# First MLP of a three-stage kernel: raw words of w_out in their own place, its conversion a block sooner, and another spread of conversion steps

## The chip, the cores and the metric

The kernel runs on one core of a Trainium2 chip. The metric is the time on the device in microseconds, lower is better; before the change the median of three runs is 873.08 us (871.41 to 873.17).

## What is computed

Three stages follow each other: an attention with a memory (4 x 8 heads, 576 tokens, 64 wide), a first MLP with a softmax gate and a layer norm, and a second, gated MLP. The weights come as 64-bit floats. The change lies in the first MLP and in what is woven into it:

```python
h = x @ w_in                      # 2304 x 512 @ 512 x 1024
e = np.exp(h - np.max(h, -1))
solu = h * e / (e.sum(-1) + 1e-9)
ln = (solu - mu) / np.sqrt(var + 1e-6) * g_ln   # mu, var over the 1024
x = ln @ w_out                    # 1024 x 512
# second MLP
gate = 1 / (1 + np.exp(-(x @ w_gate)))
return (gate * (x @ w_val)) @ w_out2
```

## The kernel before

**The stages.** Attention ends at about 222 us, the first MLP (`Moe1.run`) lasts until 453 us, the second (`Moe2`) until the end. Matmuls run on a hi and a lo part of each operand (three matmuls for one), so each tile that TensorE (PE) reads is made by a copy that rounds (hi, on ScalarE, ACT) and a subtraction (lo, on VectorE, DVE, or GpSimd, POOL). [...]

**The first MLP.** 18 blocks of 128 tokens, t = 0 to 17; blocks 0 and 1 are begun within the attention's last steps by hooks (`hooks`, keys of a step in the attention's written order). From block 2 on the loop in `run` writes for block t, in this order: 24 matmuls `h` (L665) in two halves with the transposes `pl` of block t-2 (L712) between them; ACT's `parts(t-2, 0)` (L720), `norm(t-1)` (L702); DVE's `max` (L678); ACT's `exp` (L683); DVE's `parts(t-2, 1)` (L722, the lo part of lnT) and `mul` (L687 to L689); ACT's `square` (L694); and then products `po` (L731) of a group of three finished blocks with w_out, whose results go into X (L738). A half is 12 matmuls of 384 columns. `xsplit` (L652, L654) makes the x of a later block. Each engine works through its instructions in the order in which they are written. There are two buffers each for `h`, `pl` and `po`: `h(t)` waits for `square(t-2)`, `pl(t)` for the lo part of block t-1.

**w_out of the first MLP.** Eight row chunks c. 0 and 1 are converted in the attention (`ex16` to `ex19`), 2 to 7 by the five functions of `w_out` (load, one, two, three, four; lists `outs[c][0]` to `[4]`), one chunk in each block from 2 to 7, the last step (woh, L640, on ACT) a block after the others. All buffers of this conversion and of the second MLP's conversion (`raw`, `ex`, `M`, `hi`, `ho`) come from one pool `cv`. The tags `raw` of `rawwo2` and `rawwo3` lie where the attention's tiles were, and the loads wait until these are read for the last time.

**The second MLP's conversion.** 96 steps (`conv`) prepare its weights; they run in blocks 8 to 16 between the first MLP's own work: `later` holds the steps that are due, `go(n)` runs n of them. 16 come due at t = 8, then 10 in each block.

**The last part.** After block 17, `last()` does the remaining products, with the second MLP's first differences (L1008, POOL) and their hi and lo parts (L1018, L1022) beside them.

## Time and profile before

| | us |
|---|---|
| median of the runs shown | 873.08 (871.41 to 873.17) |
| profiled execution | 873.04 |
| its span | 871.2 |
| PE busy in the span | 839.7 (96%) |
| DVE busy | 640.4 (74%) |
| ACT busy | 501.5 (58%) |
| POOL busy | 483.4 (55%) |
| first MLP after the attention, blocks 2 to 8 | 82.66 |
| first MLP, blocks 9 to 17 | 113.55 |
| rest of the first MLP | 35.00 |

A stretch is read from the start of one matmul to the start of another. A time in brackets behind an instruction is the idle time of its engine ahead of it, with what ended it. PEclk is the granted clock of TensorE as a share of full speed; a matmul of a given shape that lasts about twice its usual time ran at the lower of the two levels.

### The profile page before, as it was taken

To read this page: it belongs to the slowest core of one execution; us is meant where nothing else is said; L and a number is where in the kernel's file an instruction comes from. 1 tells how busy PE (TensorE), PEld (TensorE's weight loads), DVE (VectorE), ACT (ScalarE), POOL (GpSimd) and SP (SyncE) were. 2 spreads that over 40 slices of the span, in tenths; PEclk is the share of its full clock that TensorE was granted. 3 is DMA by queue.
4 is the path that set the end of the run, shared out by engine and by line. 5 is a ranking of instruction groups with operands and counts; after the bars stand their busy time and mean duration, and the time that the engine had idled before them with its cause. 6 is when DMAs were issued, how large, how long until landed. Compare 5 with 4: busy or idle time off the path is not lost.

```text
span 871.2 us, 14952 instructions
## 1 busy us (share of the span) xinstructions
PE 839.7 (96%) x5020; PEld 734.0 (84%) x5020; DVE 640.4 (74%) x1406; ACT 501.5 (58%) x1089; POOL 483.4 (55%) x592
## 2 busy tenths in 40 slices
PE   6999999999799999999999999999999999999998
PEld 4777777777587887877998999899899999999997
DVE  7899999996688278889537778787876444846745
ACT  5899999996588367677633446435543223423221
POOL 5687777774265187768604775685566232432111
PEclk9899999999999899999999999999999999999999
DMA  6443434430121155655429875994799874291662
GB/s 148 108 107 88 115 92 119 100 78 14 61 73 53 46 176 178 210 186 170 145 83 393 253 283 176 378 406 142 242 409 303 282 214 123 96 381 53 220 251 97
DMA packets 132412, 153.56 MB, mean 176 GB/s; under 512 B 67184, under 2 KB 101232, under 8 KB 132336
## 3 DMA queue, kind: packets, MB, share of 16 engines
q1 hardware_dynamic: 132336, 152.61, 53.9%
q8 instruction: 40, 0.66, 0.3%
q14 instruction: 36, 0.29, 0.1%
HBM read 116.40 MB, written 36.18 MB: 175 GB/s over the span
## 4 chain that ended last, share of the span: by engine, by line
PE 72%; DVE 11%; ACT 7%; POOL 4%; issue 3%; DMA 2%; SPq 0%; POOLq 0%; DVEq 0%; ACTq 0%
PE s L1073 16%; PE acc L1126 16%; PE g L1073 8%; PE po L731 5%; PE x L503 5%; PE sc L394 4%; PE v L1073 4%; PE x L488 2%; ACT h L694 2%; PE sc L385 2%; ACT e L683 1%; DVE ex L130 1%; DVE ex L121 1%; DVE M L934 1%; POOL exwo L635 1%
## 5 line engine op out<-in xcount | busy, mean ns | idle before, releaser
L1126 PE MATMUL acc<-o,G 128*128 128x512 f32 x648 | 181.6, 390 | 0.2 <-DVE G L1092 0.2
L1111 POOL TENSOR_TENSOR vl<-vl,sg 128x384 f32<-128x384 f32 x36 | 37.1, 1029 | 206.4 <-ACT sg L1110 206.4
L1126 PEld LDWEIGHTS acc<-o,G 128*128 128x128 f32 x648 | 118.5, 188 | 10.2 <-DVE G L1092 0.7
L433 POOL TENSOR_SCALAR p<-p,first,cols 128x256 f32<-128x256 f32 (+3 forms) x142 | 92.0, 662 | 5.2 <-ACT ex L118 1.9
L665 PE MATMUL h<-wih,xs 128*128 128x512 f32 x288 | 86.9, 406 | 0.9 <-ACT h L694 0.9
L422 ACT ACTIVATE p<-p,nm 128x128 f32<-128x128 f32 (+2 forms) x144 | 82.7, 582 | 0.3 <-DVE nm L416 0.3
L731 PE MATMUL po<-lnT,woh 128*128 128x384 f32 x288 | 74.6, 340 | 3.7 <-ACT woh L640 3.7
L1103 ACT ACTIVATE sg<-sg 128x384 f32<-128x384 f32 x36 | 18.9, 525 | 93.9 <-DVE sg L1102 93.9
L1092 DVE TENSOR_TENSOR G<-vl,G 128x384 fp32r<-128x384 f32 x72 | 54.0, 750 | 21.5 <-ACT G L1089 21.4
L665 PEld LDWEIGHTS h<-wih,xs 128*128 128x128 f32 x288 | 53.7, 193 | 11.4 <-ACT h L694 1.3
L1089 ACT CAST G<-vl 128x384 fp32r<-128x384 f32 x72 | 37.0, 514 | 43.6 <-POOL vl L1111 34.8
L1110 ACT ACTIVATE sg<-sg 128x384 f32<-128x384 f32 x36 | 18.9, 526 | 71.0 <-DVE sg L1109 70.8
L731 PEld LDWEIGHTS po<-lnT,woh 128*128 128x128 f32 x288 | 53.0, 191 | 4.5 <-ACT woh L640 4.0
L416 DVE CUSTOM_DVE_ANT_0 p<-sc,mask 128x128 f32<-128x128 f32 (+3 forms) x128 | 54.6, 480 | 1.2 <-PE sc L394 1.0
L118 ACT ACTIVATE ex<-ex,consts 128x512 int32<-128x512 int32 (+1 forms) x56 | 36.2, 646 | 32.2 <-DVE ex L108 32.2
L121 DVE SCALAR_TENSOR_TENSOR ex<-raw,ex 128x512 int32<-128x512 int32 (+1 forms) x56 | 44.8, 799 | 7.6 <-ACT ex L118 7.6
L731 PE MATMUL po<-lnT,wol 128*128 128x384 f32 x144 | 48.9, 340 | 0.0
L906 POOL TENSOR_TENSOR M<-ex 128x256 f32<-128x256 f32 x48 | 41.0, 873 | 13.5 <-DVE ex L130 13.5
L1097 DVE TENSOR_TENSOR u<-s,p 128x384 f32<-128x384 f32 x36 | 20.0, 556 | 36.3 <-PE s L1073 34.7
L920 POOL TENSOR_TENSOR M<-M 128x256 f32<-128x256 f32 x48 | 45.5, 958 | 1.1
L341 POOL TENSOR_TENSOR G<-E,zm 128x640 f32<-128x640 f32 x16 | 25.0, 1563 | 37.3 <-DVE E L338 32.6
L665 PE MATMUL h<-wil,xs 128*128 128x512 f32 x144 | 45.7, 399 | 0.0
(711 smaller groups left out, 2485.3 us busy)
## 6 DMA issues: line engine op xcount, KB each, us to landing
o<-scro SPq DMA_DIRECT2D x36, 512.0 KB, 4.2
scrg<-hi SPq DMA_DIRECT2D x36, 256.0 KB, 4.7
scrg<-M SPq DMA_DIRECT2D x36, 256.0 KB, 4.7
raw<-in_moe_w_val_dram SPq DMA_DIRECT2D x12, 512.0 KB, 5.4
raw<-in_moe_w_gate_dram SPq DMA_DIRECT2D x12, 512.0 KB, 4.1
raw<-in_moe_w_out_dram SPq DMA_DIRECT2D x12, 512.0 KB, 5.3
scro<-ho SPq DMA_DIRECT2D x12, 512.0 KB, 2.7
out_dram<-X SPq DMA_DIRECT2D x18, 256.0 KB, 2.0
```

The source lines that it names most:

```text
L121: nc.vector.scalar_tensor_tensor(ex, raw[:, :, 1], -0x80000000, ex, ALU.bitwise_and, ALU.bitwise_or)
L416: nc.vector.tensor_tensor_reduce(p, x, m, -1.0, 3.0e38, ALU.add, ALU.min, nm)
L422: nc.scalar.activation(p, p, AF.Exp, bias=nm, scale=-1.0, accum_out=self.sum[n % 2][:, c, 0:1])
L433: eng.tensor_scalar(p, p, r["rs"][:, c : c + 1], og, ALU.mult, ALU.mult)
L503: nc.tensor.matmul(r["x", g][64 * hh : 64 * hh + 64, c0 : c0 + src.shape[1]], r["vt"][:, c : c + D], src, start=False, stop=j == 0,)
L665: lambda s=s, w=w, j=j: nc.tensor.matmul(ph[:, j * 512 : j * 512 + 512], xs[:, s, c], self.wi[c][w][:, j * 512 : j * 512 + 512], start=(c ...
L731: nc.tensor.matmul(self.po[g, m], w[:, m * P : m * P + P], L[x][c // 4][:, c % 4], start=(c == 0 and n == 0), stop=(c == NF1 - 1 and n == 2),)
L906: nc.gpsimd.tensor_mul(out[:, sl], m[:, sl], e[:, sl])
L920: ops[i][0](*ops[i][1:])
L1073: nc.tensor.matmul(po, W[:, a, c * P : c * P + P], xb[b][:, c], start=c + i == 0, stop=c == 1 and i == 2)
L1092: nc.vector.tensor_sub(G[:, 1, hs[h]], vl[:, h], f32(G[:, 0, hs[h]]))
L1126: nc.tensor.matmul(po, G[:, x, sl], o[:, w], start=first and i == 0, stop=stop and i == 2)
```

## The change

1. **Pools.** `cv` becomes three pools: `cm` for M, `cr` for raw, `cv` for the rest. rawwo2 and rawwo3 lie elsewhere, over other tiles of the attention.
2. **Conversion of w_out one block sooner.** `outs[2][1:4]` and `outs[3][1]` stand before the loop; block t has `outs[t][4]` behind its `max`, `outs[t+1][2]` and `[3]`, the load and `[1]` of t+2.
3. **Block 1.** Its max and exp hang on an earlier attention step, mul on another; `xsplit(2)` is split around block 0's mul and square.
4. **Order on DVE.** For t < 8 the lo part (L722 twice) of block t-2 stands ahead of `max(t)`, not behind `exp(t)`.
5. **Products of group 0.** c 0 to 4 in block 5, nothing in block 6, c 5 to 7 and the two other column blocks (48 matmuls) in block 7. Block 8 is then like the others.
6. **Spread of the 96 steps.** 14 come due at t = 7, then 8 or 9 in each of the blocks 8 to 17.

```diff
@@ Moe1.run
-            outs[2][1]()
             for n in range(2):
                 self.xsplit(NFIRST + 1, n)
+            for f in outs[2][1:4]:
+                f()
+            outs[3][1]()
...
-                if t >= NF1:
-                    n = min(len(conv), 16 + (len(conv) - 16) * (t - NF1) // (NBLK - NF1 - 2))
+                if t >= NF1 - 1:
+                    n = 14 + (len(conv) - 14) * (t - NF1 + 1) // (NBLK - NF1)
                     later += conv[done:n]
                     done = n
-                go(3)
+                if t >= NF1:
+                    go(3)
...
                 self.parts(t - 2, 0)
+                if t < NF1:
+                    self.parts(t - 2, 1)
                 if t > NFIRST:
                     self.norm(t - 1)
                 self.max(t)
-                if NFIRST < t < NF1:
-                    outs[t - 1][4]()
+                if t < NF1:
+                    outs[t][4]()
                 self.exp(t)
-                go(2)
-                self.parts(t - 2, 1)
+                if t >= NF1:
+                    go(2)
+                    self.parts(t - 2, 1)
...
-                if t < NF1:
-                    outs[t][2]()
+                if t + 1 < NF1:
+                    outs[t + 1][2]()
                 self.mul(t)
...
+                pieces = self.pieces(t)
+                if t == NF1 - 1:
+                    for f, copy in pieces[:4]:
+                        f(), copy and copy()
+                    pieces = pieces[4:]
                 self.square(t)
-                if t < NF1:
-                    outs[t][3]()
+                if t + 1 < NF1:
+                    outs[t + 1][3]()
                     if t + 2 < NF1:
-                        outs[t + 2][0]()
-                    if t + 1 < NF1:
-                        outs[t + 1][1]()
+                        outs[t + 2][0]() if t + 2 > 3 else None
+                        outs[t + 2][1]()
@@ pieces
+            if t == 5:
+                return [(lambda m=m: self.product(0, m, list(range(5))), None) for m in range(2)]
+            if t == NF1 - 1:
                 return [
+                    *((lambda m=m: self.product(0, m, [5, 6]), None) for m in range(2)),
+                    *((lambda m=m: self.product(0, m, [7]), lambda m=m: self.result(0, m)) for m in range(2)),
+                    *self.halves(0)[4:],
+                ]
@@ hooks
-                lambda: m1.max(0, A), lambda: m1.exp(0, A), split(2),
-                lambda: [f(0, A) for f in (m1.mul, m1.square)], lambda: m1.norm(0),
+                lambda: m1.max(0, A), lambda: m1.exp(0, A), lambda: m1.xsplit(2, 0, A),
+                lambda: m1.mul(0, A), lambda: m1.square(0, A), lambda: m1.xsplit(2, 1, A),
             ],
+            (NP, "cv_b"): [lambda: m1.max(1, A), lambda: m1.exp(1, A)],
+            (NP, "x0_c"): [lambda: m1.mul(1, A), lambda: m1.norm(0)],
...
-            for f in (m1.max, m1.exp, m1.mul, m1.square):
-                f(1, A)
+            m1.square(1, A)
@@ pools
-        with pool("cv", side="right") as cv:
+        with pool("cm", side="right") as cm, pool("cr", side="right") as cr, pool("cv", side="right") as cv:
+            cv = Pools(M=cm, raw=cr, ex=cv, hi=cv, ho=cv)
```

On DVE, around block 1's maximum (`h1`, reduced by L678 into `first`; `wo0` is the converted w_out chunk 0, `X` the attention's output), the rows before are:

```order
L121 SCALAR_TENSOR_TENSOR ex17_3530<-raw17_3492,ex17_3530 128x256
L130 SCALAR_TENSOR_TENSOR ex17_3530<-raw17_3492,consts_63,ex17_3530 128x256
L144 COPY X_67<-x15_0_3588 128x4x64
L557 TENSOR_TENSOR wo0_74<-ex16_3527,wo0_74 128x256
L557 TENSOR_TENSOR wo0_74<-ex17_3530,wo0_74 128x256
L144 COPY X_67<-x15_1_3595 128x5x64
L678 TENSOR_REDUCE first_103<-h1_3549 128x1
L687 TENSOR_REDUCE first_103<-first_103 128x1
L688 RECIPROCAL first_103<-first_103 128x1
L689 SCALAR_TENSOR_TENSOR e1_3625,first_103<-h1_3549,first_103,e1_3625 128x1024
```

and after:

```order
L121 SCALAR_TENSOR_TENSOR ex17_3530<-raw17_3492,ex17_3530 128x256
L130 SCALAR_TENSOR_TENSOR ex17_3530<-raw17_3492,consts_63,ex17_3530 128x256
L678 TENSOR_REDUCE first_103<-h1_3549 128x1
L144 COPY X_67<-x15_0_3587 128x4x64
L687 TENSOR_REDUCE first_103<-first_103 128x1
L688 RECIPROCAL first_103<-first_103 128x1
L689 SCALAR_TENSOR_TENSOR e1_3612,first_103<-h1_3549,first_103,e1_3612 128x1024
L557 TENSOR_TENSOR wo0_74<-ex16_3527,wo0_74 128x256
L557 TENSOR_TENSOR wo0_74<-ex17_3530,wo0_74 128x256
L144 COPY X_67<-x15_1_3594 128x5x64
```

The maximum now stands directly behind chunk 0's last L130, `mul(1)` (L687 to L689) follows the first L144, and the two L557 and the second L144, which stood ahead of all four, come after them.

On DVE, at block 2 (`exwo2` and `exwo3` are chunks 2 and 3 of w_out in conversion, `rawwo` their raw words, `pl0` the transposes of block 0, `h2` the block's matmul result), the rows before are:

```order
L108 TENSOR_SCALAR exwo2_3728<-rawwo2_3724 128x512
L111 TENSOR_SCALAR exwo2_3728<-rawwo2_3724 128x512
L678 TENSOR_REDUCE consts_63<-h2_3734 128x1
L722 TENSOR_TENSOR lnT0_3747<-pl0_0_3748,lnT0_3747 128x4x128
L722 TENSOR_TENSOR lnT0_3747<-pl0_1_3753,lnT0_3747 128x4x128
L687 TENSOR_REDUCE consts_63<-consts_63 128x1
L688 RECIPROCAL consts_63<-consts_63 128x1
L689 SCALAR_TENSOR_TENSOR e2_3773,consts_63<-h2_3734,consts_63,e2_3773 128x1024
L121 SCALAR_TENSOR_TENSOR exwo2_3728<-rawwo2_3724,exwo2_3728 128x512
L130 SCALAR_TENSOR_TENSOR exwo2_3728<-rawwo2_3724,consts_63,exwo2_3728 128x512
```

and after:

```order
L108 TENSOR_SCALAR exwo2_3737<-rawwo2_3730 128x512
L111 TENSOR_SCALAR exwo2_3737<-rawwo2_3730 128x512
L121 SCALAR_TENSOR_TENSOR exwo2_3737<-rawwo2_3730,exwo2_3737 128x512
L130 SCALAR_TENSOR_TENSOR exwo2_3737<-rawwo2_3730,consts_63,exwo2_3737 128x512
L108 TENSOR_SCALAR exwo3_3746<-rawwo3_3732 128x512
L111 TENSOR_SCALAR exwo3_3746<-rawwo3_3732 128x512
L722 TENSOR_TENSOR lnT0_3762<-pl0_0_3763,lnT0_3762 128x4x128
L722 TENSOR_TENSOR lnT0_3762<-pl0_1_3768,lnT0_3762 128x4x128
L678 TENSOR_REDUCE consts_63<-h2_3749 128x1
L687 TENSOR_REDUCE consts_63<-consts_63 128x1
L688 RECIPROCAL consts_63<-consts_63 128x1
L689 SCALAR_TENSOR_TENSOR e2_3793,consts_63<-h2_3749,consts_63,e2_3793 128x1024
```

The whole of chunk 2's work and the first half of chunk 3's now stand ahead of the lo part of block 0, and the maximum of block 2 behind it.

On PE, from the end of block 7's second half on (`po0_0` to `po0_3` are group 0's four column blocks, `woh7` the hi part of chunk 7), the rows before are:

```order
L731 MATMUL po0_0_4000<-lnT0_3747,woh5_3714 128x384 x2
L731 MATMUL po0_0_4000<-lnT0_3747,wol5_3715 128x384
L731 MATMUL po0_1_4013<-lnT0_3747,woh5_3714 128x384 x2
L731 MATMUL po0_1_4013<-lnT0_3747,wol5_3715 128x384
L665 MATMUL h8_4174<-wih0_83,xs8_4072 128x512 x2
L665 MATMUL h8_4174<-wil0_84,xs8_4072 128x512 x2
L665 MATMUL h8_4174<-wih0_83,xs8_4072 128x512 x2
```

and after:

```order
L731 MATMUL po0_0_4018<-lnT0_3762,woh5_3720 128x384 x2
L731 MATMUL po0_0_4018<-lnT0_3762,wol5_3721 128x384
L731 MATMUL po0_0_4018<-lnT0_3762,woh6_3722 128x384 x2
L731 MATMUL po0_0_4018<-lnT0_3762,wol6_3723 128x384
L731 MATMUL po0_1_4034<-lnT0_3762,woh5_3720 128x384 x2
L731 MATMUL po0_1_4034<-lnT0_3762,wol5_3721 128x384
L731 MATMUL po0_1_4034<-lnT0_3762,woh6_3722 128x384 x2
L731 MATMUL po0_1_4034<-lnT0_3762,wol6_3723 128x384
L731 MATMUL po0_0_4018<-lnT0_3762,woh7_3724 128x384 x2
L731 MATMUL po0_0_4018<-lnT0_3762,wol7_3725 128x384
L731 MATMUL po0_1_4034<-lnT0_3762,woh7_3724 128x384 x2
L731 MATMUL po0_1_4034<-lnT0_3762,wol7_3725 128x384
```

Before, `h8` follows chunk 5. After, chunks 6 and 7 of the first two column blocks stand ahead of it, and behind these rows, still ahead of `h8`, all chunks of the third and fourth column block.

## Rows read from the trace of the kernel before

**Rows 1.** Stretches: from-to, length, PE, PEld, DVE, ACT, POOL busy, PEclk, DMA share.
```profile
222.19:304.85 82.66, 72.90 (x359) 63.56 (x357) 53.78 (x102) 56.13 (x94) 32.17 (x52) 0.94 0.18 58
304.85:418.40 113.55, 105.67 (x543) 92.36 (x543) 97.06 (x141) 78.75 (x138) 88.15 (x111) 0.98 0.56 179
418.40:453.40 35.00, 35.00 (x209) 34.94 (x209) 14.67 (x18) 16.50 (x28) 13.46 (x18) 1.00 0.30 100
```

**Rows 2.** PE in time: start, us, line, out<-in, count, [idle before <-releaser].
```profile
228.72 1.63 PE L712 MATMUL pl<-ident,e 128*128 128x128 f32 x8 [3.47 <-DVE e L689]
...
238.58 1.23 PE L712 MATMUL pl<-ident,e 128*128 128x128 f32 x8 [1.70 <-DVE lnT L722]
...
285.26 1.01 PE L731 MATMUL po<-lnT,woh 128*128 128x384 f32 x2 [3.69 <-ACT woh L640]
...
288.48 2.12 PE L731 MATMUL po<-lnT,wo 128*128 128x384 f32 x6
```

**Rows 3.** PE in time, second stretch; first three rows begin h9, products, h10.
```profile
304.85 0.63 PE L665 MATMUL h<-wih,xs 128*128 128x512 f32 x2
...
311.23 0.51 PE L731 MATMUL po<-lnT,woh 128*128 128x384 f32 x2
...
317.50 0.63 PE L665 MATMUL h<-wih,xs 128*128 128x512 f32 x2
...
333.96 1.41 PE L712 MATMUL pl<-ident,e 128*128 128x128 f32 x8 [2.08 <-DVE lnT L722]
335.01 1.20 PE L665 MATMUL h<-wih,xs 128*128 128x512 f32 x2
```

**Rows 4.** DVE in time around blocks 1 and 2.
```profile
219.02 0.48 DVE L130 SCALAR_TENSOR_TENSOR ex<-raw,consts,ex 128x256 f32<-128x256 uint16 x1
...
223.32 0.76 DVE L557 TENSOR_TENSOR wo<-ex,wo 128x256 fp32r<-128x256 f32 x2 [3.19 <-ACT wo L553]
...
224.40 1.22 DVE L678 TENSOR_REDUCE first<-h 128x1 f32<-128x1024 f32 x1
...
227.28 1.28 DVE L689 SCALAR_TENSOR_TENSOR e<-h,first,e 128x1024 f32<-128x1024 f32 x1
...
231.48 1.05 DVE L130 SCALAR_TENSOR_TENSOR ex<-raw,consts,ex 128x256 f32<-128x256 uint16 x1
...
235.94 0.43 DVE L108 TENSOR_SCALAR exwo<-rawwo 128x512 int32<-128x512 int32 x1 [1.70 <-DMA rawwo<-in_moe_w_out_dram]
...
240.71 0.80 DVE L121 SCALAR_TENSOR_TENSOR exwo<-rawwo,exwo 128x512 int32<-128x512 int32 x1
```

**Rows 5.** SP in time: where rawwo's loads are issued.
```profile
232.56 25.86 SPq L105 DMA_DIRECT2D rawwo<-in_moe_w_out_dram  x5
```

**Rows 6.** ACT in time: exp(2), exp(7), and woh7's cast.
```profile
237.87 1.11 ACT L683 ACTIVATE e<-h,consts 128x1024 f32<-128x1024 f32 x1 [3.11 <-DVE consts L678]
...
276.79 1.11 ACT L683 ACTIVATE e<-h,consts 128x1024 f32<-128x1024 f32 x1
...
284.59 0.62 ACT L640 CAST woh<-exwo 128x512 fp32r<-128x512 f32 x1 [1.35 <-POOL exwo L635]
```

**Rows 7.** The stretch from max(9) to max(16), columns as in rows 1.
```profile
316.78:410.56 93.78, 87.28 (x449) 76.44 (x448) 82.20 (x123) 66.60 (x117) 72.23 (x92) 0.98 0.60 194
```

**Rows 8.** DVE in time, second stretch.
```profile
316.78 1.21 DVE L678 TENSOR_REDUCE consts<-h 128x1 f32<-128x1024 f32 x1
...
320.10 1.27 DVE L722 TENSOR_TENSOR lnT<-pl,lnT 128x512 fp32r<-128x512 f32 x2
...
323.48 0.42 DVE L108 TENSOR_SCALAR ex<-raw 128x512 int32<-128x512 int32 x1
...
367.45 0.96 DVE L108 TENSOR_SCALAR ex<-raw 128x512 int32<-128x512 int32 x1
```

**Rows 9.** POOL's second difference T2 and ACT's cast of it, in time.
```profile
428.27 1.99 POOL L1008 TENSOR_TENSOR Tt<-X,Tt 128x384 f32<-128x384 f32 x2
...
432.47 0.85 ACT L1018 CAST xt2h<-Tt 128x768 fp32r<-128x768 f32 x1
```

More of the change, by code (lines that the diff above doesn't have):

```diff
@@ L767, in run @@
             for t in range(NFIRST, NBLK):
-                if t >= NF1:
-                    n = min(len(conv), 16 + (len(conv) - 16) * (t - NF1) // (NBLK - NF1 - 2))
+                if t >= NF1 - 1:
+                    n = 14 + (len(conv) - 14) * (t - NF1 + 1) // (NBLK - NF1)
                     later += conv[done:n]
                     done = n
-                go(3)
+                if t >= NF1:
+                    go(3)
                 mms = [f for c in range(NC) for f in self.h(t, c)]
-                at = len(mms) if t == NF1 else len(mms) // 2
-                for f in mms[:at]:
-                    f()
-                if t == NF1:
-                    outs[t - 1][4]()
-                    for f, copy in self.pieces(0):
-                        f(), copy and copy()
+                for f in mms[: len(mms) // 2]:
+                    f()
                 for x in range(2):
                     self.trans(t - 2, x)
-                for f in mms[at:]:
+                for f in mms[len(mms) // 2 :]:
                     f()
                 self.parts(t - 2, 0)
+                if t < NF1:
+                    self.parts(t - 2, 1)
                 if t > NFIRST:
@@ L800, in run @@
                     self.xsplit(t + 2, 1)
+                pieces = self.pieces(t)
[3 more added lines that the diff above has]
+                    pieces = pieces[4:]
                 self.square(t)
[L802 to L803 removed]
+                if t + 1 < NF1:
+                    outs[t + 1][3]()
                     if t + 2 < NF1:
[L805 to L808 removed]
+                        outs[t + 2][0]() if t + 2 > 3 else None
+                        outs[t + 2][1]()
+                for f, copy in pieces:
                     f(), copy and copy()
@@ L813, in pieces @@
         def pieces(self, t):
-            if t == 0:
+            if t == 5:
+                return [(lambda m=m: self.product(0, m, list(range(5))), None) for m in range(2)]
+            if t == NF1 - 1:
                 return [
-                    (lambda m=m: self.product(0, m, [6, 7]), lambda m=m: self.result(0, m)) for m in range(2)
-                ] + self.halves(0)[4:]
+                    *((lambda m=m: self.product(0, m, [5, 6]), None) for m in range(2)),
+                    *((lambda m=m: self.product(0, m, [7]), lambda m=m: self.result(0, m)) for m in range(2)),
+                    *self.halves(0)[4:],
+                ]
             if t < NF1:
-                cs = {5: list(range(4)), 6: [4], 7: [5]}.get(t)
-                return [(lambda m=m: self.product(0, m, cs), None) for m in range(2)] if cs else []
+                return []
             g, i = divmod(t - 5, GB)
@@ L1273, in pool, with tile @@
         return tc.tile_pool(name=nm, bufs=bufs, reuse_waits="tile", **kw)
+    class Pools(dict):
+        def tile(self, shape, dtype, tag, **kw):
+            return self[tag].tile(shape, dtype, tag=tag, **kw)
     scr = ctx.enter_context(tc.tile_pool(name="scr", bufs=1, space=bass.MemoryType.DRAM))
```

2 lines of the change are left out of this document (removed).

## The prediction

> **What bounds the kernel now.** I read first the busy table: PE is busy for 96% of the span, so only time that PE loses can be won. By the table of stretches it loses it in two places around the attention's end: 82.66 us in which PE is busy 72.90 at a granted clock of 0.94, and 113.55 us with 105.67 busy at 0.98; in the 35.00 us behind them it is busy throughout [rows 1]. To price PE's own work I take block 9, which waits for nothing: h9 starts at 304.85, its products at 311.23, h10 at 317.50 [rows 3]. So a block's 24 matmuls and its transposes cost 6.38 us, and three halves of products (36 matmuls) 6.27, or 0.174 apiece.
>
> The first stretch holds seven such blocks (h2 to h8) and 132 product matmuls: 7 x 6.38 + 132 x 0.174 = 67.6. PE loses 82.66 - 67.6 = 15.0 there. PE's rows in time show where [rows 2]: it waits 3.47 for DVE's mul(1), 1.70 for the lo part of lnT, and 3.69 for ACT's woh7, and matmuls behind the first and last of these are slow (six products in 2.12, against 6 x 0.174 = 1.04: the lower clock level). The rest is small waits and restarts.
>
> The second stretch reaches from h9's start to h17's end. Between two block ends PE has 6.38 and three halves (12.65), or two halves (6.38 + 4.18 = 10.56) in blocks 10, 13 and 16. Eight intervals, five long and three short, make 94.9; with h17's 6.38 it is 101.3, so PE loses 12.2. The loss is waits for lnT's lo part, the longest 2.08, with the next two h matmuls in 1.20 against 0.63 without the wait [rows 3]. What makes lnT late is DVE: from max(9) to max(16), seven blocks, it needs 93.78 us, 13.40 a block, and is busy for 82.20 of it [rows 7]. And 6.38 + 8 x 13.40 = 113.6 is the stretch's length: DVE's loop sets it.
>
> **Parts 1 to 4, the start.** DVE does block 1's max at 224.40, after it sat 3.19 in front of an L557 that waits for ACT; the mul ends at 227.28 + 1.28 = 228.56 [rows 4], and pl0 starts 0.16 later [rows 2]. In the new order the max can follow the L130 of 219.02 [rows 4], at 219.5. The chain from there to mul's end took 4.16, so mul ends at 223.7, before PE gets to pl0 (228.72 - 3.47 = 225.25). The 3.47 go, and the slow matmuls behind it.
>
> Next late is pl1. Before, it waits for L722 behind max(2), behind rawwo2's L108, which waited 1.70 for its load until 235.94 [rows 4]; that load was issued at 232.56 [rows 5], right when the L130 of 231.48 + 1.05 ended [rows 4], which had the old buffer. Moved, it waits for an attention matmul that ends by 222.2, so it lands before it is needed: 10 us sooner. DVE then has L557 and the conversions of w_out's chunk 1, which before lasted from 228.56 to the L557 that ended about 234.2, some 5.7. They start about 4 sooner, behind the two moved L557, so I take their end at 230.1. Six conversion instructions of rawwo2 and rawwo3 follow, four of about 0.4 and two up to 0.8 [rows 4]: until 233.2. Two L722 (1.2) and the max (1.2) end at 234.4 and 235.65, where exp(2) starts: 2.2 sooner than 237.87 [rows 6]. PE reaches pl1's place 5 us sooner and waits some 2.5 there, for DVE again; that is a new wait and stays inside the chain.
>
> From exp(2) to exp(7) the blocks come every (276.79 - 237.87) / 5 = 7.78 us [rows 6], and ACT is the engine that paces them: its work per block isn't changed, only the order. So I keep 7.78, and exp(7) starts at 274.55.
>
> **Parts 2 and 5, woh7.** Its cast now stands right ahead of exp(7), not at 284.59 behind the first steps of the second MLP's conversion and a wait for POOL of 1.35 [rows 6], so woh7 is there at 274.6 and the 3.69 shrink to a little. From it to h9's start PE has 6 + 48 + 36 product matmuls and h8: 90 x 0.174 + 6.38 = 22.0, with 0.6 for restarts: h9 starts at 297.2. Before: 304.85. **Gain 7.6.** Bounds: if exp(2) gets no sooner, h9 starts 2.2 later and 5.4 stay; if pl1's wait is gone too, 9. The seven casts (L640) stand ahead of an exp each, on ACT; exp waits if POOL's product is late.
>
> Part 5 costs PE nothing: the same matmuls, 48 of them ahead of h8 instead of behind. They hide the 14 conversion steps now at the end of block 7: 14 x 0.88 (below) = 12.3 on DVE, beside 48 x 0.174 + 6.38 = 14.7 on PE. Without that cover, max(8) is 12 later.
>
> **Part 6, the spread.** Of DVE's 13.40, the block's own work is the max (1.21) and the part from L722 to the end of xsplit (320.10 to 323.48, 3.38) [rows 8]: 4.59. The other 8.81 are ten steps: 0.881 apiece with their waits, or (82.20 / 7 - 4.59) / 10 = 0.715 without. Now 8.25 steps stand in a mean block: 4.59 + 8.25 x 0.881 = 11.86, against PE's 94.9 / 8 = 11.87. So DVE just stops being the bound. A single late block can be borne: L722 ends some 4.6 after the max starts, and PE asks for it two halves and half an h later, 4.18 + 2.8 = 7.0; that leaves 2.4 in the short blocks. The whole 12.2 could go. But the chunks of conversion aren't even, and DVE and PE run at the same pace, so I leave one wait like the longest (2.08), and half of what it drew after it, 1.2: **gain 8.9**, bounds 12.2 and, if a step gets dearer, below nothing.
>
> What a step costs depends on POOL. An L108 of the same shape takes 0.42 at 323.48 and 0.96 at 367.45 [rows 8]; a conversion's DVE instruction can be 0.54 longer. The Trainium skill (SBUF — State Buffer, "Who interferes with whom") says that DVE and GpSimd share a port pair which is an exclusive lock, and that a DVE instruction with two SBUF inputs contends with a GpSimd one that reads SBUF; by it, a denser loop on both engines would lengthen DVE's steps, and the gain could be lost as in the first rival below. The two L108 agree with that as far as they go. A step's price then lies between 0.715 and 0.881 + 0.54 = 1.42; I take 0.881, since POOL's work shrinks with the steps in a block as DVE's does.
>
> **The tail.** The 35.00 are full [rows 1]: nothing to win. To lose: steps now run in block 17, so POOL gets to T1 and T2 later; T2 ends at 430.26 and ACT casts it at 432.47 [rows 9], which leaves 2.2. I take 0.5, with 0 and 2 as bounds.
>
> **Sum.** 873.04 (the profiled run, as good as the median 873.08) - 7.6 - 8.9 + 0.5 = 857.0.
>
> **Rivals.** *DVE paces the second stretch still.* At a step of 1.1, midway to the upper bound, the loop is 13.67, 6.38 + 8 x 13.67 - 2.4 (slack) = 113.3, and only the start's gain is left: 873 - 7.6 - 0.3 + 0.5 = 865.7. For it: the long L108. Against: the mean that holds for seven blocks has such rows in it.
>
> *ACT takes the start's gain back.* If POOL's product ends after max(t), each exp waits behind its L640 as the last one did, 1.35 [rows 6]; five blocks make 6.75 of the 7.6: 863.9. It decides once POOL's product comes later than the max. Against: the product still has a whole block of time.
>
> *Slower.* DVE's step price again, but higher: from 4.59 + 8.25p = 14.57, p = 1.21, the second stretch loses the 7.1 that start and tail leave; that is six tenths of the steps' instructions moving from 0.42 to 0.96. At 1.3 the loop is 15.32 and the time 879. Against: it would be dearer than any mean here.
>
> *Nothing.* The start is only shifted and the loop paced as before: both of the first two rivals, 872.
>
> **Chances.** Forecast (853.5 to 861) 0.63, the DVE rival 0.14, the ACT rival 0.14, slower 0.04, nothing 0.05. A difference under 0.2%, 1.7 us, is no change for what can be measured here. So faster 0.91, same 0.05, slower 0.04. The range takes in the forecast with both gains in full (873 - 7.6 - 12.2 + 0.5 = 853.7) and the first two rivals: 853.5 to 866.
>
> **What would show it.** Of the changed kernel: no wait of PE for mul(1); rawwo2's load issued by about 222; exp(2) near 235.7 and exp(7) 38.9 later; no wait at woh7 over 1.5; h9 at 297. From max(9) to max(16) about 83 to 85 us, seven times 11.9, with PE waits for lnT of under 4 in sum. A loop of 12.7 or more a block, with L108 or L111 near 0.96 in most chunks, speaks for the DVE rival; exp(3) to exp(7) more than 8.5 apart, with ACT waiting for POOL at L640, for the ACT rival. I am wrong if h9 starts after 301, or if PE's waits in the last blocks move to the tail behind T1 or T2.

## The result and the profile after

The kernel after takes 859.46 us (median, 857.94 to 859.68), the kernel before 872.49 beside it; the ratio is 0.9848 (95% interval 0.9831 to 0.9865), a gain of 13.0 us. The forecast was 857.0 with a range of 853.5 to 866.

In the rows, the conversion steps are made of these lines, on tiles `ex` of 128x512: L108 and L111 take exponent and mantissa out of the raw words (DVE), L118 and a scaling turn them to floats (ACT), L121 and L130 put in sign and low bits (DVE), and POOL multiplies the two (L635 for w_out, L914 for the second MLP). From block 2's loop on, line numbers differ from those of the kernel before: POOL's products and sums L906 and L920 are L914 and L928 after, the lo part L934 is L942, and the differences L1008 and their casts L1018 are L1016 and L1026; in some of the runs below they move by a few lines more.

The busy table of the page and its row of TensorE's clock, after:

```profile
PE 834.7 (97%) x5020; PEld 731.9 (85%) x5020; DVE 631.7 (74%) x1406; ACT 501.0 (58%) x1089; POOL 481.7 (56%) x592
...
PEclk8899999999999999999999999999999999999999
```

The first MLP by stretches, after (columns as in rows 1: start of h2 to start of h9, to the first product behind h17, to the first matmul of the second MLP):

```profile
221.50:298.36 76.86, 70.95 (x359) 61.09 (x358) 58.36 (x105) 57.98 (x97) 44.37 (x66) 0.98 0.24 78
298.36:399.61 101.25, 101.25 (x541) 91.86 (x541) 79.92 (x133) 73.64 (x129) 69.40 (x92) 1.00 0.57 180
399.61:439.42 39.81, 36.95 (x209) 36.50 (x208) 17.39 (x22) 18.59 (x32) 19.93 (x24) 0.96 0.29 100
```

With the same marks the kernel before has 82.66, 113.36 and 35.09 [rows 1; there the last mark but one is 0.19 later]. So the start gains 5.80, the second stretch 12.11, and the tail loses 4.72. With 0.69 in the attention, which differs so from profile to profile (h2 starts between 220.7 and 222.8 in all of them), and 0.48 lost behind, this makes the 13.4 between the spans. The second stretch is full now: 101.25 busy of 101.25, which is the 101.3 that the prediction worked out as PE's own work.

All PE waits of 0.2 us or more from h2 to the end of the first MLP, after (start, us, line, [idle before <-releaser]):

```profile
234.11 1.71 PE L712 MATMUL pl<-ident,e 128*128 128x128 f32 x8 [3.23 <-DVE lnT L722]
...
240.07 0.74 PE L665 MATMUL h<-wih,xs 128*128 128x512 f32 x2 [0.48 <-ACT h L694]
...
247.76 0.73 PE L665 MATMUL h<-wih,xs 128*128 128x512 f32 x2 [1.01 <-ACT h L694]
...
275.27 0.62 PE L731 MATMUL po<-lnT,woh 128*128 128x384 f32 x2 [0.79 <-ACT woh L640]
...
276.09 0.44 PE L731 MATMUL po<-lnT,wol 128*128 128x384 f32 x1 [0.20 <-POOL wol L154]
...
277.26 1.32 PE L731 MATMUL po<-lnT,wo 128*128 128x384 f32 x6 [0.21 <-ACT X L738]
...
410.98 1.55 PE L731 MATMUL po<-lnT,wo 128*128 128x384 f32 x6 [2.86 <-ACT X L738]
```

The 3.47 for mul(1) and the 3.69 for woh7 [rows 2] are gone or 0.79, and the waits for lnT in the second stretch [rows 3] are gone altogether. Two long ones remain: 3.23 at pl1, and a new one of 2.86 in the tail, for a result copy (L738).

DVE in time at the start, after: max and mul of block 1, rawwo2's first conversion, two later instructions of rawwo2's and rawwo3's conversion, max(2).

```profile
218.72 1.22 DVE L678 TENSOR_REDUCE first<-h 128x1 f32<-128x1024 f32 x1
...
221.61 1.28 DVE L689 SCALAR_TENSOR_TENSOR e<-h,first,e 128x1024 f32<-128x1024 f32 x1
...
229.68 0.42 DVE L108 TENSOR_SCALAR exwo<-rawwo 128x512 int32<-128x512 int32 x1
...
230.89 0.69 DVE L121 SCALAR_TENSOR_TENSOR exwo<-rawwo,exwo 128x512 int32<-128x512 int32 x1 [0.45 <-ACT exwo L118]
...
232.51 0.95 DVE L111 TENSOR_SCALAR exwo<-rawwo 128x512 int32<-128x512 int32 x1
...
234.58 1.21 DVE L678 TENSOR_REDUCE consts<-h 128x1 f32<-128x1024 f32 x1
```

SP in time there, the issue of rawwo's loads:

```profile
218.54 0.85 SPq L105 DMA_DIRECT2D rawwo<-in_moe_w_out_dram  x2
```

ACT in time, exp(2) and exp(7):

```profile
235.82 1.11 ACT L683 ACTIVATE e<-h,consts 128x1024 f32<-128x1024 f32 x1 [1.13 <-DVE consts L678]
...
275.13 1.11 ACT L683 ACTIVATE e<-h,consts 128x1024 f32<-128x1024 f32 x1
```

Max(1) follows the last L130 directly and is 5.7 us sooner than in [rows 4] (5.0 counted from h2's start). The loads are issued at 218.54, not at 232.56 [rows 5], and DVE no longer waits for their words. Exp(2) stands at 235.82 (forecast 235.65), exp(7) at 275.13 (274.55), h9 at 298.36 (297.2).

DVE's maxima in the second stretch, after: of blocks 9, 10, 11, 13 and 16, then the step in front of the last, and max(17).

```profile
306.16 1.21 DVE L678 TENSOR_REDUCE consts<-h 128x1 f32<-128x1024 f32 x1
...
317.57 1.22 DVE L678 TENSOR_REDUCE consts<-h 128x1 f32<-128x1024 f32 x1 [2.13 <-PE h L665]
...
328.13 1.23 DVE L678 TENSOR_REDUCE consts<-h 128x1 f32<-128x1024 f32 x1 [1.05 <-PE h L665]
...
353.41 1.23 DVE L678 TENSOR_REDUCE consts<-h 128x1 f32<-128x1024 f32 x1 [2.99 <-PE h L665]
...
391.05 1.21 DVE L678 TENSOR_REDUCE consts<-h 128x1 f32<-128x1024 f32 x1
...
403.23 0.69 DVE L942 TENSOR_TENSOR M<-M,hi 128x512 fp32r<-128x512 f32 x1 [2.71 <-POOL M L928]
...
403.84 1.22 DVE L678 TENSOR_REDUCE consts<-h 128x1 f32<-128x1024 f32 x1
```

From max(9) to max(16) it takes 84.89 us, against 93.78 [rows 7]; and DVE now waits for PE in front of three maxima (2.13, 1.05, 2.99). Without these 6.17 its loop is (97.68 - 6.17) / 8 = 11.44 us. Less the block's own 4.59 [rows 8], that is 6.85 for some 8.13 steps (65 lie between max(9) and max(17)): 0.843 a step, where 0.881 was taken. DVE has stopped being the bound, except in block 17: there max(17) starts at 403.84 though h17 ended at 399.61.

Where the tail goes, after. First POOL in time, block 16's last small instruction and the conversion's sums:

```profile
399.19 0.77 POOL L698 TENSOR_SCALAR consts<-consts 128x1 f32<-128x1 f32 x1
...
401.76 2.75 POOL L928 TENSOR_TENSOR M<-M 128x256 f32<-128x256 f32 x3
```

Then ACT in time, square(17) and the copies behind it:

```profile
409.32 1.12 ACT L694 ACTIVATE h<-e,consts 128x1024 f32<-128x1024 f32 x1 [0.94 <-DVE e L689]
...
410.47 0.84 ACT L738 COPY X<-po 128x384 f32<-128x384 f32 x2
```

Three conversion steps stand ahead of max(17). The last of them waits 2.71 for POOL's sums (L928), which stand on POOL behind block 16's small L698 and a product. So max(17), mul(17) and square(17) are late; ACT copies the first result of block 17's products only behind square(17), at 410.47; and the products of the third column block, which need that PSUM buffer, wait for it.

### The profile page after: what moved, and what is told of

It is laid out like the page before. It is cut to its first block, busy times and chain, and to the rows that moved or that the text cites. A ratio compares the mean times of both kernels' runs of the same rounds, so it can differ in the third digit from the quotient of the medians.

```text
span 857.8 us, 14952 instructions
## 1 busy us (share of the span) xinstructions
PE 834.7 (97%) x5020; PEld 731.9 (85%) x5020; DVE 631.7 (74%) x1406; ACT 501.0 (58%) x1089; POOL 481.7 (56%) x592
## 4 chain that ended last, share of the span: by engine, by line
PE 78%; DVE 6%; ACT 5%; POOL 4%; DMA 4%; issue 2%; SPq 1%; POOLq 0%; ACTq 0%; DVEq 0%
PE s L1081 15%; PE acc L1134 15%; PE po L731 8%; PE g L1081 8%; PE h L665 6%; PE x L503 5%; PE sc L394 4%; PE v L1081 4%; PE x L488 2%; PE sc L385 1%; ACT h L694 1%; PE pl L712 1%; DMA raw<-in_moe_w_val_dram 1%; DMA gv0s<-scrg 1%; ACT e L683 1%
## 5 line engine op out<-in xcount | busy, mean ns | idle before, releaser
L914 POOL TENSOR_TENSOR M<-ex 128x256 f32<-128x256 f32 x48 | 41.8, 891 | 18.1 <-DVE ex L130 18.1
L118 ACT ACTIVATE ex<-ex,consts 128x512 int32<-128x512 int32 (+1 forms) x56 | 36.2, 647 | 22.7 <-DVE ex L108 22.7
L121 DVE SCALAR_TENSOR_TENSOR ex<-raw,ex 128x512 int32<-128x512 int32 (+1 forms) x56 | 41.6, 742 | 9.9 <-ACT ex L118 9.8
L928 POOL TENSOR_TENSOR M<-M 128x256 f32<-128x256 f32 x48 | 42.5, 896 | 1.2
```

What stands on the lines that cost most here:

```text
L121: nc.vector.scalar_tensor_tensor(ex, raw[:, :, 1], -0x80000000, ex, ALU.bitwise_and, ALU.bitwise_or)
L914: nc.gpsimd.tensor_mul(out[:, sl], m[:, sl], e[:, sl])
L928: ops[i][0](*ops[i][1:])
```

## The experiments

All times are medians beside runs of the kernel before, which stood at 872.2 to 872.5. The stretches of each run's profile, with the marks used above:

| kernel | time | start | second | tail |
|---|---|---|---|---|
| before | 872.5 | 82.66 | 113.36 | 35.09 |
| after | 859.46 | 76.86 | 101.25 | 39.81 |
| e1: no steps ahead of max(17) | 859.7 | 76.88 | 101.25 | 38.59 |
| e2: after, old spread | 866.46 | 76.90 | 113.33 | 35.08 |
| e3: before, new spread | 876.4 | 82.31 | 110.47 | 41.74 |
| e5: after, old block 1 | 862.87 | 80.87 | 101.26 | 39.77 |
| e6: after, one pool | 862.26 | 78.85 | 101.25 | 39.92 |
| e9: after, max ahead of lo | 860.2 | 75.78 | 101.26 | 41.00 |
| e11: after, woh casts on DVE | 858.62 | 76.13 | 101.25 | 38.25 |
| f1: last copy ahead of square(17) | 859.91 | 76.85 | 101.26 | 40.61 |
| f2: f1 and last lo parts on DVE | 857.72 | 76.88 | 101.25 | 37.57 |
| g1: f2, e9, e11 and products spread | 856.1 | 75.62 | 101.26 | 37.67 |
| e3b: before, 16 steps first | 876.36 | 82.23 | 111.24 | 42.14 |
| g2: after, no steps in block 7 | 871.01 | 76.85 | 111.97 | 40.32 |

In the kernels made from the kernel after, start and second stretch repeat to 0.1 us where an edit doesn't touch them, so they tell small effects apart that the medians, with runs some 1 to 3 us apart, don't. The tail doesn't repeat like that: where nothing in it was edited (after, e5, e6, e9, e11) it takes 39.81, 39.77, 39.92, 41.00 and 38.25, by the clock that follows the same wait (last section). So two tails of single profiles that are less than 2.8 apart say little by their length. In the kernels made from the kernel before, an untouched start differs by up to 0.4.

**The parts of the start.** First, part 3 undone (e5):

```diff
-            (NP, "cv_b"): [lambda: m1.max(1, A), lambda: m1.exp(1, A)],
-            (NP, "x0_c"): [lambda: m1.mul(1, A), lambda: m1.norm(0)],
...
-            m1.square(1, A)
+            for f in (m1.max, m1.exp, m1.mul, m1.square):
+                f(1, A)
```

> The kernel after with part 3 undone: block 1's maximum, exp and mul behind the conversions as in the kernel before, xsplit(2) not split. Theory (DVE's chain of mul(1), chunk 1's conversion, chunk 2's, L722, max(2) leads to exp(2), and ACT's pace of 7.8 us per block carries exp(2) on to h9): PE waits 3.5 for mul(1) again, exp(2) comes 3.8 later, at about 239.6, and so does h9; time 863.3. Rival (the wait of 3.23 at pl1, which stands behind it in the kernel after, takes it up): 859.5 to 860.

862.87. Its PE wait for mul(1), from PE in time:

```profile
228.57 1.84 PE L712 MATMUL pl<-ident,e 128*128 128x128 f32 x8 [3.47 <-DVE e L689]
```

And its max(2), from DVE in time:

```profile
238.92 1.21 DVE L678 TENSOR_REDUCE consts<-h 128x1 f32<-128x1024 f32 x1
```

The wait of 3.47 is back to the digit; counted from h2's start, max(2) comes 3.8 later than in the kernel after, as expected, and the start is 4.0 longer. The chain from mul(1) to exp(2) and on to h9 carries the whole delay, as the theory said; the wait at pl1 shrinks to 1.73 but doesn't take it up.

Part 1 undone (e6):

```diff
-        with pool("cm", side="right") as cm, pool("cr", side="right") as cr, pool("cv", side="right") as cv:
+        with pool("cv", side="right") as cv:
...
-            cv = Pools(M=cm, raw=cr, ex=cv, hi=cv, ho=cv)
```

> The kernel after with part 1 undone: one pool for all buffers of the conversions, so rawwo2 and rawwo3 lie where they did before. Theory: their loads are issued only when the last L130 of ex19 has ended, about 228.1, and land some 3.4 later, at 231.5; DVE wants the words at 229.7, so it waits 1.8 there, exp(2) and all behind it come 1.8 later, and the time is 861.3. Rival (DVE has other work or the load lands in time): 859.5.

862.26. The issue of rawwo's loads, from SP in time:

```profile
229.36 0.80 SPq L105 DMA_DIRECT2D rawwo<-in_moe_w_out_dram  x2
```

And the first conversion of them, from DVE in time:

```profile
232.89 0.43 DVE L108 TENSOR_SCALAR exwo<-rawwo 128x512 int32<-128x512 int32 x1 [1.84 <-DMA rawwo<-in_moe_w_out_dram]
```

Counted from h2's start, the load is issued 9.5 later than in the kernel after, and DVE waits 1.84 for it (1.8 expected); the start is 2.0 longer. The median is 2.8 above that of the kernel after, more than that: in the profile h2 starts 1.28 later, which differs so without any edit. So the start's 5.8 lose 4.0 without part 3 and 2.0 without part 1, each undone by itself; both lie on one chain, and the two needn't add. Parts 2 and 5, the earlier woh7, weren't run apart; what they bring by themselves stays open.

Part 4 undone (e9):

```diff
                 self.parts(t - 2, 0)
-                if t < NF1:
-                    self.parts(t - 2, 1)
...
                 if t >= NF1:
                     go(2)
-                    self.parts(t - 2, 1)
+                self.parts(t - 2, 1)
```

> The kernel after with part 4 undone: in blocks 2 to 7 the lo part of lnT (two L722) stands behind the maximum and exp again. Theory (exp(2) starts ACT's chain of 7.8 us per block, and the L722 stand in front of it): exp(2) comes 1.2 sooner, at about 234.6, h9 too, though PE waits 1.2 longer at pl1: 858.3. Rival (PE, which waits for the L722 at pl1, is the one that carries the delay on): h3 ends 1.2 later, and so does all behind it: 860.7.

860.2, which the medians can't tell from 859.46. The stretches can: the start is 1.08 shorter, the tail 1.19 longer. So part 4 costs the start 1.1 us, as the theory had it (the maximum, not the lo part, leads to exp(2)). The tail, in which nothing was edited, is told of below.

The casts on DVE (e11):

```diff
                 hi, lo = wo[c]
-                nc.scalar.copy(hi, m)
+                nc.vector.tensor_copy(hi, m)
```

> The kernel after with the casts of woh2 to woh7 (L640) on DVE instead of ACT, at the same place in the order. Theory (ACT paces blocks 2 to 7: some 7.2 of 7.8 us busy): each block gets up to 0.6 shorter, PE's waits for square (0.48 and 1.01) and for woh7 (0.79) shrink, h9 comes 2 to 3 sooner: about 857. Rival (the pace is a chain from a block's matmuls over max, exp, mul, square back to the matmuls two blocks on, of which the cast is no part): the pace stays at 7.7 to 7.8, 859.5.

858.62, but the start got only 0.73 shorter, not 2 to 3. From exp(2) on the blocks come after 7.32, 7.34 and 7.82 us, then after 8.66 and 7.16. ACT paced the first of them, since they got shorter by 0.4; in their place exp(3) and exp(4) now wait 0.31 each for DVE's maximum. Block 6 comes late since PE does 30 products and 24 h matmuls, 5.2 + 6.4, behind h5. So ACT's pace of 7.78 was the bound of the blocks but not by much; DVE's maximum and, in block 6, PE are next.

**The spread, and what it stands on.** The old spread in the kernel after (e2):

```diff
-                if t >= NF1 - 1:
-                    n = 14 + (len(conv) - 14) * (t - NF1 + 1) // (NBLK - NF1)
+                if t >= NF1:
+                    n = min(len(conv), 16 + (len(conv) - 16) * (t - NF1) // (NBLK - NF1 - 2))
```

> The kernel after with the old spread of the 96 steps: 16 come due in block 8, then 10 in each block, none in block 17. Theory (the spread alone makes the second stretch short, by 12.1 us, and lengthens the tail by 4.6): h9 starts as in the kernel after, the second stretch takes about 113 us again with PE waits for lnT's lo part, the tail 35.2, and the time is 859.5 + 12.1 - 4.6 = 867.0. Rival (the second stretch profits from the earlier start and the calm block 8, not from the spread): about 860 to 862.

866.46, against 867.0 expected. The second stretch is 113.33 and the tail 35.08, both as before the change, and the start keeps its 76.90. The stretch from max(9) to max(16) (columns as in rows 1):

```profile
310.25:403.35 93.10, 85.36 (x445) 74.41 (x444) 83.24 (x122) 66.72 (x117) 72.74 (x92) 1.00 0.62 198
```

It takes 13.30 a block, nearly the 13.40 of the kernel before, so ten steps a block make DVE pace the stretch, also with the earlier start. The tail's loss belongs to the spread. This run takes two things away at once, the thinner spread and the 14 steps in block 7, and can't tell them apart; the next three ask for that.

The new spread alone in the kernel before (e3), where the first 22 steps fall into block 8:

```diff
                 if t >= NF1:
-                    n = min(len(conv), 16 + (len(conv) - 16) * (t - NF1) // (NBLK - NF1 - 2))
+                    n = 14 + (len(conv) - 14) * (t - NF1 + 1) // (NBLK - NF1)
```

> The kernel before with the new spread alone: 22 steps in block 8, then 8 or 9 in each block up to 17; nothing else of the change. Theory: the second stretch falls to 101 to 103 us, the tail grows to near 40, the start stays at 82.7: 872.5 - 12.1 + 4.6 = 865.0. Rival (the spread needs the 14 steps in block 7, and 22 in block 8 make DVE late for blocks 9 to 11): the second stretch stays over 106 and the time over 868.

876.4: slower than the kernel before (ratio 1.0047, 1.003 to 1.0063), and the rival was right. PE's wait in h10, from PE in time:

```profile
326.47 1.94 PE L712 MATMUL pl<-ident,e 128*128 128x128 f32 x8 [7.51 <-DVE lnT L722]
```

And max(9) from DVE in time, though h9 had ended at 309.77:

```profile
321.94 1.21 DVE L678 TENSOR_REDUCE consts<-h 128x1 f32<-128x1024 f32 x1
```

DVE works on the pile until 321.94; PE waits 7.51. From there the stretch runs without a wait, but what it gains (2.9) is less than the tail's 6.6.

Was it the 22? With 16 in block 8, as in the kernel before, and 80 spread over blocks 9 to 17 (e3b):

```diff
                 if t >= NF1:
-                    n = min(len(conv), 16 + (len(conv) - 16) * (t - NF1) // (NBLK - NF1 - 2))
+                    n = 16 + (len(conv) - 16) * (t - NF1) // (NBLK - NF1 - 1)
```

> The kernel before with 16 steps in block 8 as it has them, and then 80 steps evenly over blocks 9 to 17 (8 or 9 each). The run with 22 steps in block 8 was slower than before: PE waited 7.51 for lnT in block 10, since DVE worked on the 22 until max(10) at 321.9, and only then ran at the pace of the kernel after. Theory (the pile in block 8 is its trouble, a thin spread from block 9 on isn't): no wait over 2.5 in blocks 9 to 16, the second stretch near 104, the tail near 39, time 866 to 868. Rival (without block 7's cover any spread leaves DVE late): 872 or more.

(The maximum at 321.94 that this text calls max(10) is max(9), as the rows of the blocks behind it show.) 876.36. The theory fell: the second stretch gains 2.1, not 9. DVE in time: block 6's lo part in block 8, max(9), and a later conversion step.

```profile
297.04 1.29 DVE L722 TENSOR_TENSOR lnT<-pl,lnT 128x512 fp32r<-128x512 f32 x2 [13.42 <-ACT lnT L720]
...
314.83 1.21 DVE L678 TENSOR_REDUCE consts<-h 128x1 f32<-128x1024 f32 x1
...
370.51 0.98 DVE L108 TENSOR_SCALAR ex<-raw 128x512 int32<-128x512 int32 x1 [3.70 <-DMA raw<-in_moe_w_out_dram]
```

PE's longest wait in the stretch, behind that step:

```profile
372.24 1.27 PE L712 MATMUL pl<-ident,e 128*128 128x128 f32 x8 [3.75 <-DVE lnT L722]
```

Two things are seen. DVE stands 13.42 us in front of block 6's lo part, because in the kernel before, in block 8 alone, the transposes stand on PE behind all of h8 and 60 products, and everything queued on DVE stands behind it; so max(9) comes at 314.83, 5.5 after h9's end (309.29), even with 16 steps. In the kernel before it is as late: 316.78 [rows 8], with h9's end at 311.23 [rows 3]. In the kernel after it is 1.4 late (306.16 and 304.73). And the steps then wait for other things: 3.70 for a load of raw words, with a PE wait of 3.75 behind it.

At last the kernel after, where block 8 is like the others, without its 14 steps in block 7 (g2):

```diff
-                if t >= NF1 - 1:
+                if t >= NF1:
                     n = 14 + (len(conv) - 14) * (t - NF1 + 1) // (NBLK - NF1)
```

> The kernel after with no conversion step in block 7: 22 come due in block 8, then 8 or 9 in each block as in the kernel after. The products of group 0 keep their place ahead of h8, so that block 8 is like the others. Theory (the spread pays only because 14 steps are done on DVE while PE does 48 products and h8): DVE does 14 steps more in block 8, 12 us that the slack of some 2.4 to 4.5 can't take, PE waits 6 to 8 in block 9 or 10, with slow matmuls after it, and the time is 867 to 869. Rival (the products' place is what counts, since DVE no longer stands 13.4 us in front of block 6's lo part as it does in the kernel before): 860 to 862.

871.01. It was dearer than the 867 to 869 of the theory. DVE in front of max(8), from DVE in time:

```profile
293.43 1.22 DVE L678 TENSOR_REDUCE consts<-h 128x1 f32<-128x1024 f32 x1 [12.90 <-PE h L665]
```

It has nothing to do there for 12.90 us, while PE does the products and h8; in the kernel after the 14 steps fill that time and max(8) waits for nothing. Its PE wait in h10, from PE in time:

```profile
323.25 1.94 PE L712 MATMUL pl<-ident,e 128*128 128x128 f32 x8 [8.20 <-DVE lnT L722]
```

Its max(9), from DVE in time:

```profile
318.72 1.21 DVE L678 TENSOR_REDUCE consts<-h 128x1 f32<-128x1024 f32 x1
```

And its second stretch (columns as in rows 1):

```profile
299.49:411.46 111.97, 103.78 (x541) 93.74 (x541) 88.49 (x139) 77.08 (x135) 82.63 (x104) 0.95 0.55 177
```

Max(9) is 12.9 late (h9 ends at 305.86), PE waits 8.20, and the granted clock of the stretch is 0.95, not 1.00; 10.7 of the 12.1 are lost. Beside 22 steps in block 8 the place of the products alone is worth nothing (111.97, against 110.47 in e3); it is worth what is done on DVE meanwhile. So the thinner spread alone isn't enough (e3, e3b, g2): the gain of the second stretch needs the 14 steps done under the 48 products that now stand ahead of h8. That it needs the thinner spread as well is argued from DVE's 13.30 a block at ten steps (e2) against PE's 11.87; the cover with ten steps a block wasn't run. Nor was an even spread from block 8 on, with neither the cover nor a pile in block 8, so g2's 10.7 is the price of both together.

**The tail.** The three steps ahead of max(17) taken away (e1):

```diff
-                if t >= NF1:
+                if NF1 <= t < NBLK - 1:
                     go(3)
```

> The kernel after, but in block 17 no conversion step stands ahead of the block's matmuls and maximum; the three that stood there run behind the maximum with the others. In the trace of the kernel after, PE loses 4.6 us behind block 17: it waits 2.86 for a result copy (L738), which on ACT stands behind square(17), and the matmuls after the wait are slow. Theory: the copy is late because max(17) is late (403.84, though h17 ended at 399.6), and max(17) is late because DVE waits 2.71 us in front of it for a conversion step's POOL sum. Then max(17) follows h17 at once, the wait of 2.86 goes with its slow matmuls, and the time is about 855.0 (854 to 856). Rival: the copy is late since ACT is full with casts of the conversion, whatever DVE does: the wait stays between 2 and 3 and the time at 859.5.

859.7. Both were wrong: the wait of 2.86 is gone (0.3 is left), but the time is the same. The tail of the profile, 38.59 with no slow matmul, is no shorter than the unedited one of e11, 38.25, which has none either. PE's wait in the tail, from PE in time:

```profile
422.30 1.33 PE L731 MATMUL po<-lnT,wo 128*128 128x384 f32 x6 [2.78 <-DVE lnT L722]
```

And the cast of T2, from ACT in time:

```profile
419.82 0.83 ACT L1026 CAST xt2h<-Tt 128x768 fp32r<-128x768 f32 x1 [4.53 <-POOL Tt L1016]
```

The next limit is block 17's lnT. Its L720 stands on ACT behind the cast of T2, the second of POOL's differences, and that cast waits 4.53 for POOL. The copy ahead of square(17) instead (f1):

```diff
+                if t == NBLK - 1:
+                    for f, copy in pieces:
+                        f(), copy and copy()
+                    pieces = []
                 self.square(t)
```

> The kernel after, but block 17's products and the copy of their result (L738) are written ahead of square(17), so that ACT makes the copy before it waits for mul(17); the conversion steps of block 17 keep their places. PE's order stays. The run without steps ahead of max(17) lost the wait of 2.86 at the third product, but PE then waited 2.78 for block 17's lnT, behind POOL's differences, which came later. Theory now (the copy is one cause, and the differences are the next in line only if they come later than in the kernel after): here POOL's differences stay where they are in the kernel after, the wait of 2.86 falls under 0.8, the slow matmuls behind it go, and the time is 855 to 856. Rival (whatever ends first, block 17's conversion work on POOL holds the tail): a wait of 2 to 3 appears behind, 858.5 to 859.5.

859.91: the rival was right, though 0.4 dearer than it said. PE's two waits in the tail, from PE in time:

```profile
409.86 1.32 PE L731 MATMUL po<-lnT,wo 128*128 128x384 f32 x6 [0.67 <-ACT X L738]
...
422.98 1.98 PE L731 MATMUL po<-lnT,wo 128*128 128x384 f32 x6 [2.72 <-DVE lnT L722]
```

The 2.86 fell to 0.67, and 2.72 came up behind, at the same place as in e1. So two limits stand one behind the other, with nearly the same end: the copy, and T2 on POOL. Both at once (f2):

```diff
+            last = nc.vector if f == EARLY - 1 else nc.gpsimd
...
-                [lambda: hi(6, 7), hi_o, lambda: save(0, 2)], [lo_o], [lambda: lo(4, 6, nc.gpsimd), save_o],
-                [lambda: lo(6, 7, nc.gpsimd), lambda: save(4, 6)], [lambda: lo(2, 4), lambda: save(6, 7)], [lambda: save(2, 4)],
+                [lambda: hi(6, 7), hi_o, lambda: save(0, 2)], [lo_o], [lambda: lo(4, 6, last), save_o],
+                [lambda: lo(6, 7, last), lambda: save(4, 6)], [lambda: lo(2, 4), lambda: save(6, 7)], [lambda: save(2, 4)],
```

> The run with the copy ahead of square(17), and besides the lo parts (4,6) and (6,7) of the last chunk of the second MLP on DVE instead of POOL (three POOL instructions, 2.13 us, ahead of its first difference). In the run with the early copy alone the wait for the copy fell from 2.86 to 0.67, but PE then waited 2.72 for block 17's lnT: its ACT part L720 stands behind the cast of T2 (xt2h, 419.62), which waits 3.59 for POOL. Theory (two limits stand one behind the other, the copy and POOL's T2): T2 comes 2.1 sooner, the wait of 2.72 falls to about 0.6, its slow matmuls go, and the time is 855.5 to 856.5. Rival (POOL's differences wait for something else, a buffer that the last save holds): the wait stays over 2 and the time at 859 to 860.

857.72. The tail is 37.57. Its two PE waits, from PE in time:

```profile
410.04 1.31 PE L731 MATMUL po<-lnT,wo 128*128 128x384 f32 x6 [0.72 <-ACT X L738]
...
421.62 1.31 PE L731 MATMUL po<-lnT,wo 128*128 128x384 f32 x6 [1.21 <-DVE lnT L722]
```

And the first difference, from POOL in time:

```profile
414.47 1.99 POOL L1021 TENSOR_TENSOR Tt<-X 128x384 f32<-128x384 f32 x2 [1.09 <-DMA scro<-ho]
```

The waits are 0.72 and 1.21. Counted from h17's end, the difference comes only 0.6 sooner than in f1, not 2.1: it waits 1.09 for the save of `ho` (a DMA); it reads nothing of `ho`, so what it waits for is the place. The rival's mechanism is there, though not at its full size. What is left of the tail's loss is 2.5. The median is 1.7 below that of the kernel after; of the 2.2 between the two tails a part is the clock, since the slow matmuls of the one (0.96) are missing in the other (1.00).

With the start's edits besides (g1), and group 0's products spread as chunks 0 to 2 in block 5 and 3 and 4 in block 6:

```diff
-            if t == 5:
-                return [(lambda m=m: self.product(0, m, list(range(5))), None) for m in range(2)]
+            if t in (5, 6):
+                cs = [0, 1, 2] if t == 5 else [3, 4]
+                return [(lambda m=m: self.product(0, m, cs), None) for m in range(2)]
```

> The run above with three edits of blocks 2 to 7: the maximum ahead of the two L722 (exp(2) came 1.1 sooner so, counted from exp(0)), the casts of woh2 to woh7 on DVE (h9 0.7 sooner), and group 0's products spread as chunks 0 to 2 in block 5 and 3 and 4 in block 6, so that block 5 doesn't take 11.6 us on PE. Theory (exp(2) and ACT's pace carry to h9): exp(8) comes 81 to 82 behind exp(0) instead of 83.6, and the time is 2 below the run above: 853.5 to 854.5. Rival (PE itself paces the blocks by now, since it waits only 1.5 in blocks 3 to 7): within 0.7 of the run above.

856.1 (ratio to the kernel before 0.982, 0.9805 to 0.9834), the fastest of all; the start is 1.26 shorter than in f2, where 2 was expected. Its PE waits 4.84 at pl1 and 0.64 later in the start, and none for square or woh7. The 1.6 between the medians of f2 and g1 lies between theory and rival.

## Why the prediction was right, and where it wasn't

**The time** lay 2.5 above the forecast, but its terms were off by more and cancelled in part: 7.6 + 8.9 - 0.5 was forecast, 5.8 + 12.1 - 4.7 came. That the total came so near is in part luck: the second stretch gave 3.2 more than forecast, start and tail 6.0 less.

**Start, 7.6 forecast, 5.8 measured.** The mechanism was right step by step: mul(1) off PE's path, rawwo2's load off DVE's, exp(2), ACT's pace, woh7. The runs that undo parts 3 and 1 bring back 4.0 and 2.0. The 1.8 that is missing, counted from h2's start: exp(2) 0.86 later than worked out, 0.60 of it since the six conversion instructions of rawwo2 and rawwo3 were costed as if none waited or was slowed (one waits 0.45 for ACT, an L111 takes 0.95), and the rest since chunk 1's work on DVE ends later; the five blocks 0.39 longer, as block 6 waits for PE; and exp(7) to h9 0.58 longer, most of it PE's late start on woh7 (0.14 behind exp(7)) and the waits of 0.20 and 0.21 right behind it. Part 4 is no part of this: its two L722 stood in the prediction's chain at 1.2, and e9 gives 1.1 for them.

**Second stretch, 8.9 forecast, 12.1 measured.** DVE's loop against PE's own 94.9 decided it, as worked out, once the cover of the next paragraph is there; the old spread, without the cover, brings the old 113.3 back (e2). The 3.3 held back for one late block wasn't needed: DVE's step cost 0.843 and it waits for PE. The rival by which a step gets dearer didn't come: of 28 L108 and L111 in the second stretch after, 8 take more than 0.8 us; of 32 before, 16. But the loop didn't get denser either. DVE's busy share of the stretch went from 85% (97.06 of 113.55 [rows 1]) to 79%, and POOL's from 78% to 69%, so what a denser loop does isn't shown. The sentence of the Trainium skill on two SBUF inputs, which stood beside that rival (SBUF — State Buffer, "Who interferes with whom"), isn't about an L108 or L111, which read one tile; the lock of the ports in the same section agrees with the rows. All 24 long ones run beside one of POOL's products, sums or lo parts, and of the 36 others 30 run beside none of these, the other six beside a part of one.

**The cover, "they hide the 14 conversion steps".** It was named with its price, max(8) 12 later without it; g2 shows the price a block on: max(9) comes 12.9 behind h9's end, against 1.4 with it, and that makes a PE wait of 8.20 and 10.7 us of the stretch. The sum put the whole gain down to the spread, though, and 865 was expected of the spread alone in the kernel before (e3); it is 876.4.

**Tail, 0.5 forecast with bounds 0 and 2, 4.7 measured.** This is the term that was mis-sized, for a step that the prediction left out. The prediction asked only when POOL gets to T1 and T2. It didn't follow the three steps that now stand ahead of max(17) on DVE, what waits behind that maximum (mul, square, and on ACT the copy behind square), and who needs the copy: PE's products of the third column block, for there are only two PSUM buffers for `po`. The T2 term itself was real too, and hidden behind the copy: e1 and f1 uncover it at 2.7 to 2.8. What holds POOL in f2, a buffer that a save must leave first, wasn't in the prediction at all. Its own sign of being wrong, that PE's waits move to the tail behind T1 or T2, came in part: a wait moved there, but behind a result copy.

**The rivals.** ACT as the giver-back: block spacing stayed at 7.7 to 7.8 but for block 6, and ACT's waits for POOL ahead of the casts are 0.15 at most in blocks 3 to 7. *Slower* and *nothing* did not come.

## What to carry to other kernels

Work that is thinned out in a loop has to go somewhere, and it lands at the ends: follow each step that is newly put into the last iteration through the queue of its engine to the buffer that the next stage needs. Thinning pays only if the loop starts without a backlog: ask what each engine does while another has a long run of its own (here 14 steps under 48 matmuls), for without that cover, and with the 14 steps in a pile behind it, 10.7 of the 12.1 us were lost. When a wait is removed and the time stays, look for the next one in the same stretch before giving up the first theory; two limits that end together show only one of themselves.
